# Tiles that 512-column products read moved to multiples of 1024 bytes, and the opening products of zeros taken out

## The chip, the cores and the metric

One core of a Trainium2 chip runs the whole program in one launch. The metric is the device time of one execution in microseconds (us); the median of three runs of the kernel before is 1070.89 us. The engines are named as the profile names them: PE (TensorE's matmuls), PEld (its weight loads), DVE (VectorE), ACT (ScalarE), POOL (GpSimd), SP (SyncE, which issues the DMAs).

## The reference

Three stages in float32, one after the other. B = 4, H = 8, S = 576, D = 64; 4 x 576 = 2304 tokens of 512 features; d_ff = 2048.

```python
scores = scale * np.matmul(q, k.transpose(0, 1, 3, 2))        # causal, softmax
local = np.matmul(a, v)
mem_out = mem_ret / mem_norm                                  # phi(q) @ M_prev over phi(q) . z_prev
x = g * mem_out + (1 - g) * local
...
h = x @ w_in;  r = np.maximum(h, 0.0);  y = (s * (r * r) + b) @ w_out      # first layer
...
h = y @ w_in2;  g = h * np.tanh(softplus(h));  out = g @ w_out2            # second layer
```

## The kernel before

Every large product is made of three: each operand is split into a high and a low float32r part, and hi*hi, hi*lo and lo*hi are added in PSUM. `W[layer, "wih"/"wil"/"woh"/"wol", r]` are the weights' parts (w_in high and low, w_out high and low), four tiles of 512 columns each.

- **Attention** makes x in units of one batch and head; scores are `a` tiles, L469 to L474, transposes L533, products with V L561.
- **First layer.** Tokens go in five blocks of 256 (`blocks1`, j = 0 to 4) and then two of 512 ("big"). `first` makes h = x @ w_in for one 128-wide slice fc of d_ff: 12 products through `mm_in` (L699), whose moving operand is `xh` or `xl` in a small block and `yh` or `yl` in a big one, and whose stationary operand is a slice of `wih` or `wil`. `y_part` (L763) multiplies the result, `gh` and `gl` (in a big block two halves of a tile that takes the rings `xh` and `xl`), moving, by slices of `woh` and `wol`, stationary, into the block's accumulators. A small block has two accumulators of one PSUM bank each, `y0` and `y1`, each holding two 256-column results; L759 opens each with a product of a tile of zeros over all its 512 columns. A big block has four accumulators.
- **Second layer.** Blocks of 512, 512, 512, 512 and 256 tokens (`blocks2`). `mish` makes h (L699 again, moving `yh` or `yl`, stationary `wih` or `wil`); ACT applies Mish, DVE splits the result into a tile `raw` (three slices of four) or `gg` (every fourth). `o_part` (L847) multiplies: stationary a 128-wide slice of `raw` or `gg`, moving 512 columns of `woh` or `wol`. On PE four products of h and four of o alternate.
- `column_sums` adds all of the first layer's w_out up on DVE (L672, L674), and one product with a tile of ones (L692) sums over the partitions; it gives a bias of the second layer.

The order of every engine's queue is found at build time by `Plan`, which simulates the steps with fixed costs and priorities. Buffers are slots of named rings; `yh`, `yl` have two slots each, number 0 in the pool `m2a` on the right-hand end of SBUF and number 1 in the pool `m2b` on the left. The first-layer big blocks and the second layer's blocks 0, 2 and 4 take slot 0; blocks 1 and 3 take slot 1. `raw` has three slots, all on the right; `gg` one, on the left. Until about 85 us `Plan` also puts fill products (`zero_product`, L940) into PE's idle time.

The few lines on the fill and on the opening of an accumulator:

```python
def zero_product():
    if not idle:
        idle.append(ps_y.tile([P, 512], F32, tag="y1_0", name="idle"))
    nc.tensor.matmul(idle[0][:, :256].rearrange("p (k n) -> p k n", n=P), zeros,
                     zeros.unsqueeze(1).to_broadcast([P, 2, P]), start=True, stop=True)
plan.fill = (7.0, 85.0, 0.12, zero_product)
```

Of the kernel before, what the change touches and what calls it, by code (L numbers as in the profile page):

```python
# [9 lines left out]
F32 = mybir.dt.float32  # L10
F32R = mybir.dt.float32r
# [3 lines left out]
AF = mybir.ActivationFunctionType  # L15
# [4 lines left out]
P = 128  # L20
# [3 lines left out]
PE, ACT, DVE, POOL, DMA = range(5)  # L24
# [26 lines left out]
def act_us(n, extra=0):  # L51
    return 0.094 + 0.00083 * n + 0.093 * extra


def dve_us(n, fast=False):
    return 0.068 + (0.00052 if fast else 0.00104) * n
# [61 lines left out]
class Plan:  # L118
# [29 lines left out]
    def add(self, engine, us, prio, f, r=(), w=(), after=(), keep=(), share=1.0):  # L148


        bufs = list({id(b): b for b in (*r, *w, *keep) if b.ring is not None}.values())
        new = [b for b in bufs if b.maker is None]
        waits = {id(s): s for b in r for s in b.writers}
        waits.update((id(s), s) for s in after)
        s = Step(engine, us, prio, f, list(waits.values()), bufs, new)
        s.share = share
        s.left = len(waits)
        for x in waits.values():
            x.next.append(s)
        for b in bufs:  # L160
            b.users += 1
            if b.maker is None:
                b.maker = s
            elif id(b.maker) not in waits:
                b.maker.next_start.append(s)
                s.left += 1
        for b in w:
            b.writers.append(s)
        self.steps.append(s)
        return s  # L170
# [100 lines left out]
def attention_then_two_ffn(ctx: ExitStack, tc: tile.TileContext, qk, qz, vm, beta,  # L271
# [3 lines left out]
    nc = tc.nc  # L275
    B, H = qk.shape[:2]
    NQ, D = qz.shape[3] - 1, qz.shape[4]
# [20 lines left out]
    add = plan.add  # L298

    const = ctx.enter_context(tc.tile_pool(name="const", bufs=1))  # L300
# [6 lines left out]
    mask = const.tile([P, SP], BF16, name="mask")  # L307
    nc.gpsimd.memset(mask[:, :SP - P], 0.0)
    make_causal_mask(nc, mask[:, SP - P:], MASKED)
    zeros = const.tile([P, P], F32R, name="zeros")  # L310
    ones = const.tile([P, P], F32, name="ones")
    igate = const.tile([P, 2, H], F32, name="igate")
    sb = const.tile([P, 2], F32, name="sb")
    bcs = const.tile([P, NCC], F32, name="bcs")
# [16 lines left out]
    nc.vector.tensor_scalar_min(igate[:, 1], igate[:, 1], 80.0)  # L331
    nc.scalar.activation(igate, igate, AF.Exp)
    nc.vector.tensor_scalar_add(igate, igate, 1.0)
    nc.scalar.copy(zeros, mask[:, :P])
    nc.scalar.activation(ones, mask[:, :P], AF.Copy, bias=1.0)


    ps_h = ctx.enter_context(tc.tile_pool(name="ps_h", bufs=1, space=PSUM))
    stage = ctx.enter_context(tc.tile_pool(name="stage", bufs=1, side="right"))
    first_layer = ExitStack()  # L340
    m1 = first_layer.enter_context(tc.tile_pool(name="m1", bufs=1))
# [6 lines left out]
    R = {}  # L348

    def rings(pool, after=None, fifo=True, **sizes):  # L350
        for nm, n in sizes.items():
            R.setdefault(nm, Ring(nm, fifo)).more(pool, n, after)
# [14 lines left out]
    def unit(b, h, prio, groups=(TA, TB), place=None):  # L367
# [47 lines left out]


        ex = Buf(R["ex"], [P, NQ, D])
        nm = Buf(R["nm"], [P, NQ])
        lo_t, n_t = tiles[0], len(tiles)
        mine = slice(lo_t, lo_t + n_t)  # L420

# [242 lines left out]

    def column_sums(prio, begin):

        total, ps = Buf(R["total"], [P, 512]), Buf(R["h"], [P, 512])

        def more(r, j, nm):
            x = W[1, nm, r].t[:, j, :].bitcast(F32)  # L670
            if r == j == 0 and nm == "wol":
                nc.vector.tensor_tensor(total.t, W[1, "woh", 0].t[:, 0, :].bitcast(F32), x, op=ALU.add)  # L672
            elif r + j:
                nc.vector.tensor_tensor(total.t, total.t, x, op=ALU.add)  # L674

        for r in range(NR):
            for j in range(FPR):
                def pair(r=r, j=j):
                    more(r, j, "woh")
                    more(r, j, "wol")  # L680

                add(DVE, dve_us(512) * (2 if r + j else 1), prio, pair, [W[1, "woh", r], W[1, "wol", r]] + [total] * (r + j > 0), [total],
                    after=[begin] * (r + j == 0))

        def pick():
            for ec in range(NCC):
                nc.vector.tensor_tensor_reduce(total.t[:, ec * P:(ec + 1) * P], ps.t[:, ec * P:(ec + 1) * P], ident, 1.0, 0.0,
                                               ALU.mult, ALU.add, bcs[:, ec:ec + 1])
            nc.vector.tensor_scalar(bcs, bcs, sb[:, 1:2], None, op0=ALU.mult)

        plan.steps[-1].lag = 12.0
        add(PE, 0.87, prio, lambda: nc.tensor.matmul(ps.t, ones, total.t, start=True, stop=True), [total], [ps])  # L692
        add(DVE, 1.0, prio, pick, [ps, total], [sums_in, total])

    def mm_in(ph, layer, xh, xl, fc, part):
# [54 lines left out]
    def y_part(j, fc, acc, t, gh, gl, gh_bufs, gl_bufs, prio):  # L750
        r, jj = fc // FPR, fc % FPR
        n = blocks1[j][1]
        big = n > N1
        per = 512 // n

        def y(part):
            if fc == 0 and part == 0 and not big:
                for a in acc:
                    nc.tensor.matmul(a.t.rearrange("p (k n) -> p k n", n=P), zeros,  # L759
                                     zeros.unsqueeze(1).to_broadcast([P, 4, P]), start=True, stop=False)  # L760
            x, nm = ((gh, "woh"), (gh, "wol"), (gl, "woh"))[part]
            for ec in range(NCC):
                nc.tensor.matmul(acc[ec // per].t[:, (ec % per) * n:(ec % per + 1) * n],  # L763
                                 W[1, nm, r].t[:, jj, ec * P:(ec + 1) * P], t(x),
                                 start=(big and fc == 0 and part == 0),
                                 stop=(fc == NFC - 1 and part == 2 and ec % per == per - 1))

        for part in range(3):
            need = [*(gl_bufs if part == 2 else gh_bufs), W[1, "wol" if part == 1 else "woh", r]]
            add(PE, 0.48 if not big else 0.908, prio, lambda part=part: y(part), need + (acc if fc or part else []), acc,  # L770
                keep=[gh[0]])
# [22 lines left out]
    m2a, m2b, ps_or, ps_ol = [], [], [], []  # L794
# [77 lines left out]
    for h in range(H):  # L872
        unit(0, h, PRE_A + STEP_A * h, (TA,), PLACE_A[h % 4])
    for h in range(H):
        unit(0, h, PRE_B + STEP_B * h, (TB,), PLACE_B[h])
    raws = [raw_buf(i // 8, i % 8) for i in range(len(pieces))]
    weight_bufs(1)
    start = 0.0
# [3 lines left out]
    for i in range(3 * H):  # L882
        unit(1 + i // H, i % H, UNIT0 + UNIT * i)

    opened = add(NONE, 0.0, 0.0, open_second, after=attention_steps)
    rings(m2a, opened, raw=1, yr=4, yh=1, yl=1, g=2, total=1)
    rings(ps_or, opened, o0=1, o1=1, o2=1, o3=1)
    seq = [(j, fc) for j in range(NB1) for fc in range(NFC)]

# [5 lines left out]
    for i in range(len(seq) + LAG1):  # L895
        if i < len(seq):
            j, fc = seq[i]
# [6 lines left out]
        if i >= LAG1:  # L904
            j, fc = seq[i - LAG1]
# [3 lines left out]
    for p in pieces:  # L909
        convert(2, CONV2, *p, Buf(R["raw"], [P, 1024], I32), [opened])  # L910
    column_sums(700.0, begin_sums)
    weight_bufs(2)
    closed = add(NONE, 0.0, 0.0, close_first, after=list(plan.steps))
# [8 lines left out]
    for i in range(len(seq) + LAG2):  # L922
        if i < len(seq):
            blk, fc = seq[i]
# [4 lines left out]
        if i >= LAG2:  # L929
            blk, fc = seq[i - LAG2]  # L930
# [4 lines left out]
    idle = []  # L935

    def zero_product():
        if not idle:
            idle.append(ps_y.tile([P, 512], F32, tag="y1_0", name="idle"))
        nc.tensor.matmul(idle[0][:, :256].rearrange("p (k n) -> p k n", n=P), zeros,  # L940
                         zeros.unsqueeze(1).to_broadcast([P, 2, P]), start=True, stop=True)

    plan.fill = (7.0, 85.0, 0.12, zero_product)
    with tc.manual_schedule():
        plan.run()
# [42 lines left out]
```

## Time and profile before

| | |
|---|---|
| median of 3 runs | 1070.89 us (1070.43 to 1073.95) |
| the profiled execution, its own time | 1072.33 us |
| span in its profile, first to last instruction | 1070.5 us |
| PE busy | 1041.9 us, 97% of the span, 6021 instructions |
| DVE, ACT, POOL busy | 665.2, 534.7, 217.0 us |

The span is what the profile's clocks run over; the execution's own time lies 1.8 us above it. A product's time in the profile is from its start to its modelled end, and successive products overlap; how fast PE goes is read from the starts of successive products, or from how many stand in a stretch in which PE has no idle time.

### The profile page before, as it was taken

How to read it: one execution, taken by the hardware profiler on the slowest of the kernel's cores; microseconds unless marked ns; L12 is line 12 of the kernel's file. 1: busy time of each engine (PE TensorE's matmuls, PEld its weight loads, DVE VectorE, ACT ScalarE, POOL GpSimd, SP SyncE). 2: the span in 40 equal slices, each digit the busy share in tenths (PEclk: the TensorE clock that was granted, in tenths of full speed). 3: DMA queues.
4: the chain of work that ended last, by engine and by line, in shares of the span. 5: the costliest groups of instructions: out<-in, count | busy, mean ns of one | idle time of the engine just before them, and what ended most of it. 6: DMA issues, size and time to landing. Idle time of an engine off the chain costs nothing.

```text
span 1070.5 us, 17570 instructions
## 1 busy us (share of the span) xinstructions
PE 1041.9 (97%) x6021; PEld 897.9 (84%) x6021; DVE 665.2 (62%) x1962; ACT 534.7 (50%) x1268; POOL 217.0 (20%) x337
## 2 busy tenths in 40 slices
PE   7999998999999999999999999999999999999998
PEld 5667787999999999998768878888888888888887
DVE  7899999999999999856986565422311322222122
ACT  6887896878788888755345454312111211111111
POOL 5753443333223332213233200000000000000000
PEclk9999999999999999999999999999999999999999
DMA  8654552334323332267366754200200100010010
GB/s 268 180 171 142 172 180 80 113 103 137 94 86 90 122 93 82 67 191 209 121 190 192 245 188 148 79 1 2 77 1 1 42 19 1 0 40 1 1 40 20
DMA packets 52073, 106.66 MB, mean 100 GB/s; under 512 B 6672, under 2 KB 27664, under 8 KB 51984
## 3 DMA queue, kind: packets, MB, share of 16 engines
q1 hardware_dynamic: 51552, 105.54, 31.7%
q8 instruction: 47, 0.77, 0.3%
q14 instruction: 42, 0.34, 0.1%
q10 hardware_dynamic: 432, 0.01, 0.0%
HBM read 82.97 MB, written 22.54 MB: 99 GB/s over the span
## 4 chain that ended last, share of the span: by engine, by line
PE 76%; DVE 11%; DMA 3%; issue 2%; ACT 2%; POOL 1%; SPq 0%; DVEq 0%; ACTq 0%; POOLq 0%
PE h L699 31%; PE o L847 19%; PE y L763 10%; PE a L561 5%; PE a L533 4%; PE o L763 3%; PE a L473 2%; PE a L474 2%; DVE total L674 2%; DMA raw<-w_in_d 1%; DVE w L637 1%; DVE w L636 1%; DMA w_out_d<-w 1%; DVE Pt L478 1%; POOL w L639 1%
## 5 line engine op out<-in xcount | busy, mean ns | idle before, releaser
L836 ACT ACTIVATE g<-h 128x512 f32<-128x512 f32 (+1 forms) x80 | 44.5, 556 | 319.7 <-PE h L699 297.4
L837 DVE CAST raw<-g 128x512 fp32r<-128x512 f32 (+1 forms) x60 | 24.0, 401 | 214.5 <-ACT g L836 166.4
L847 PE MATMUL o<-woh,raw 128*128 128x512 f32 x432 | 119.2, 394 | 0.0
L699 PE MATMUL h<-yh,wih 128*128 128x512 f32 (+1 forms) x448 | 115.0, 379 | 3.1 <-DVE g L743 3.1
L699 PE MATMUL h<-yh,wil 128*128 128x512 f32 (+1 forms) x448 | 114.7, 378 | 0.0
L699 PE MATMUL h<-yl,wih 128*128 128x512 f32 (+1 forms) x448 | 114.7, 378 | 0.0
L639 POOL TENSOR_TENSOR w<-w,raw 128x512 int32<-128x512 int32 x54 | 75.0, 1388 | 163.9 <-DVE w L637 123.2
L699 PEld LDWEIGHTS h<-yh,wih 128*128 128x128 f32 x448 | 81.3, 188 | 22.3 <-DVE g L743 5.2
L490 POOL TENSOR_SCALAR Pt<-ex,nm 128x64 f32<-128x64 f32 x148 | 72.1, 500 | 126.6 <-DVE nm L439 64.9
L699 PEld LDWEIGHTS h<-yl,wih 128*128 128x128 f32 x448 | 81.7, 188 | 17.5
L699 PEld LDWEIGHTS h<-yh,wil 128*128 128x128 f32 x448 | 81.7, 188 | 17.5
L847 PEld LDWEIGHTS o<-woh,raw 128*128 128x128 f32 x432 | 79.2, 188 | 17.0
L487 ACT ACTIVATE Pt<-Pt,mx 128x64 f32<-128x64 f32 (+4 forms) x148 | 81.7, 553 | 20.7 <-DVE mx L478 20.2
L533 PE MATMUL a<-ident,Pt 128*128 128x128 f32 x432 | 66.1, 280 | 5.9 <-POOL Pt L504 2.4
L541 DVE TENSOR_TENSOR PTl<-a,PTh 128x128 fp32r<-128x128 f32 (+1 forms) x144 | 63.9, 481 | 1.0 <-ACT PTh L538 0.6
L478 DVE CUSTOM_DVE_ANT_0 Pt<-a,mask 128x320 f32<-128x320 f32 (+3 forms) x148 | 59.8, 419 | 7.4 <-PE a L469 4.2
L847 PE MATMUL o<-wol,raw 128*128 128x512 f32 x216 | 59.8, 394 | 0.0
L533 PEld LDWEIGHTS a<-ident,Pt 128*128 128x128 f32 x432 | 50.0, 143 | 10.8 <-POOL Pt L504 4.6
L538 ACT CAST PTh<-a 128x128 fp32r<-128x128 f32 (+1 forms) x144 | 54.3, 433 | 5.8 <-PE a L533 4.8
L699 PE MATMUL h<-xh,wih 128*128 128x256 f32 x320 | 52.0, 287 | 2.8 <-DVE rt L743 2.7
L763 PE MATMUL y<-gh,wol 128*128 128x256 f32 x320 | 53.1, 288 | 0.0
L763 PE MATMUL y<-gl,woh 128*128 128x256 f32 x320 | 53.0, 288 | 0.0
(195 smaller groups left out, 2327.8 us busy)
## 6 DMA issues: line engine op xcount, KB each, us to landing
qk<-in_qk SPq DMA_DIRECT2D x24, 608.0 KB, 3.8
raw<-in_w_out SPq DMA_DIRECT2D x28, 512.0 KB, 3.9
raw<-in_w_in SPq DMA_DIRECT2D x26, 512.0 KB, 4.7
qn<-in_qz SPq DMA_DIRECT2D x29, 192.0 KB, 2.4
vx<-in_vm SPq DMA_DIRECT2D x29, 160.0 KB, 2.4
out<-ot SPq DMA_DIRECT2D x18, 256.0 KB, 2.1
w_in_d<-w SPq DMA_DIRECT2D x16, 256.0 KB, 3.2
w_out_d<-w SPq DMA_DIRECT2D x16, 256.0 KB, 3.4
```

Of the source, the lines that this page charges most:

```text
L478: nc.vector.tensor_tensor_reduce(Pt[t].t[:, D + lo:D + hi], ps.t[:, :hi - lo], mask[:, SP - w + lo:SP - w + hi], -SCALE, mx.t[:, t:t + 1] ...
L487: nc.scalar.activation(Pt[t].t[:, D:w + D], Pt[t].t[:, D:w + D], AF.Exp, bias=mx.t[:, t + i:t + i + 1], scale=-1.0, accum_out=rs.t[:, t:t ...
L490: add(POOL, 0.3, lambda: nc.gpsimd.tensor_scalar(Pt[t].t[:, :D], ex.t[:, t, :], nm.t[:, t:t + 1], 1.0, op0=ALU.mult, op1=ALU.mult), [ex, n ...
L533: nc.tensor.transpose(ps.t[:, c - c0, :], Pt[t].t[:, c * P:(c + 1) * P], ident)
L538: (nc.vector.tensor_copy if dve else nc.scalar.copy)(PT[0].t[:, at_], ps.t[:, :n])
L541: nc.vector.tensor_tensor(PT[1].t[:, at_], ps.t[:, :n], PT[0].t[:, at_].bitcast(F32), op=ALU.subtract)
L561: nc.tensor.matmul(o.rearrange("p (t q) -> p t q", q=P), v, x.t[:, f[0]:f[-1] + 1:f[1] - f[0] if len(f) > 1 else 1, :], start=(c == 0 and ...
L639: add(POOL, 1.23, prio, lambda: nc.gpsimd.tensor_tensor(w.t, w.t, words()[:, :, 0], op=ALU.add), [raw, low_words, w], [w])
L699: nc.tensor.matmul(ph, W[layer, nm, r].t[:, cc, o:o + P], x[:, cc], start=(part == 0 and cc == 0), stop=(part == 2 and cc == NCC - 1))
L763: nc.tensor.matmul(acc[ec // per].t[:, (ec % per) * n:(ec % per + 1) * n], W[1, nm, r].t[:, jj, ec * P:(ec + 1) * P], t(x), start=(big and ...
L836: add(ACT, act_us(n) + 0.06, ew, lambda: nc.scalar.activation(g.t, ph.t[:, :n], AF.Mish), [ph], [g])
L847: nc.tensor.matmul(acc[i].t, gg.t[:, k, i * P:(i + 1) * P], W[2, nm, r].t[:, jj, :], start=(fc == 0 and part == 0), stop=(fc == NFC - 1 an ...
```

## The change

Where tiles lie. `zeros` and `ones` (512 bytes each) leave the constants, so that everything on the left-hand end moves down by 1024 bytes; a pool `edge` of 992 bytes is put at the right-hand end, and `nm` grows from 20 to 64 bytes. Start addresses per partition in the two built programs, as the remainder of a division by 1024:

| tiles | before | after |
|---|---|---|
| weights, `xh`, `xl`, `gh`, `gl`, `gg`, slot 1 of `yh` and `yl` (left) | 0 | 0 |
| slot 0 of `yh` and `yl`, `raw` (three slots), `yr`, `g`, `total`, `w32` (right) | 992 | 0 |
| attention's `PTh`, `PTl` | 992, 480 | 0, 512 |
| attention's `B1`, `B2` | 736, 736 | 768, 768 |

The products of zeros. L759 is gone; instead the first product into each bank of a small block has start set, and the second half of the bank is written by a product without it. The fill products multiply the bfloat16 mask's zero columns instead of a float32r tile of zeros. The tile of ones is made by ACT just before it is used, in the pool `m2a`.

```diff
-    zeros = const.tile([P, P], F32R, name="zeros")
-    ones = const.tile([P, P], F32, name="ones")
...
-    nc.scalar.copy(zeros, mask[:, :P])
-    nc.scalar.activation(ones, mask[:, :P], AF.Copy, bias=1.0)
...
+    edge = ctx.enter_context(tc.tile_pool(name="edge", bufs=1, side="right"))
+    edge.tile([P, 248], F32, name="edge")
     stage = ctx.enter_context(tc.tile_pool(name="stage", bufs=1, side="right"))
...
-        nm = Buf(R["nm"], [P, NQ])
+        nm = Buf(R["nm"], [P, 16])
...
-        total, ps = Buf(R["total"], [P, 512]), Buf(R["h"], [P, 512])
+        total, ps, ones = Buf(R["total"], [P, 512]), Buf(R["h"], [P, 512]), Buf(R["ones"], [P, 2 * P])
...
-        add(PE, 0.87, prio, lambda: nc.tensor.matmul(ps.t, ones, total.t, start=True, stop=True), [total], [ps])
+        add(ACT, act_us(P), prio, lambda: nc.scalar.activation(ones.t[:, :P], mask[:, :P], AF.Copy, bias=1.0), [], [ones], after=[begin])
+        add(PE, 0.87, prio, lambda: nc.tensor.matmul(ps.t, ones.t[:, :P], total.t, start=True, stop=True), [total, ones], [ps])
...
         def y(part):
-            if fc == 0 and part == 0 and not big:
-                for a in acc:
-                    nc.tensor.matmul(a.t.rearrange("p (k n) -> p k n", n=P), zeros,
-                                     zeros.unsqueeze(1).to_broadcast([P, 4, P]), start=True, stop=False)
...
-                                 start=(big and fc == 0 and part == 0),
+                                 start=(fc == 0 and part == 0 and ec % per == 0),
...
-    rings(m2a, opened, raw=1, yr=4, yh=1, yl=1, g=2, total=1)
+    rings(m2a, opened, raw=1, yr=4, yh=1, yl=1, g=2, total=1, ones=1)
...
-        nc.tensor.matmul(idle[0][:, :256].rearrange("p (k n) -> p k n", n=P), zeros,
-                         zeros.unsqueeze(1).to_broadcast([P, 2, P]), start=True, stop=True)
+        nc.tensor.matmul(idle[0][:, :256], mask[:, :P], mask[:, :256], start=True, stop=True)
```

The queues of DVE, POOL and SP hold the same instructions in the same order before and after. On PE, this is the opening of the second small block's accumulators (j = 1) before; names are out<-moving,stationary, and h, y are PSUM tiles:

```order
L699 MATMUL h_2550<-xl_2223,wih_0_802 128x256 x4
L699 MATMUL h_2622<-xh_2070,wih_0_802 128x256 x4
L759 MATMUL y_0_2632<-zeros 128x512
L759 MATMUL y_0_2633<-zeros 128x512
L763 MATMUL y_0_2632<-gh_2483,woh_0_483 128x256 x2
L763 MATMUL y_0_2633<-gh_2483,woh_0_483 128x256 x2
```

and now (the lines have moved up by one or two):

```order
L698 MATMUL h_2548<-xl_2221,wih_0_802 128x256 x4
L698 MATMUL h_2620<-xh_2068,wih_0_802 128x256 x4
L758 MATMUL y_0_2630<-gh_2481,woh_0_483 128x256 x2
L758 MATMUL y_0_2631<-gh_2481,woh_0_483 128x256 x2
L531 MATMUL a_2639<-ident,Pt_0_2412 128x128 x4
```

The two products of zeros are gone, in each of five such places, and nothing else on PE has changed its place. On ACT, this is the stretch in which the column sums are made, before:

```order
L629 ACTIVATE w_0_7898<-raw_7823 128x512
L742 ACTIVATE g_7905<-h_7865 128x512
L634 ACTIVATE raw_7871<-raw_7871 128x512
L629 ACTIVATE w_1_7929<-raw_7871 128x512
L745 CAST xh_7945<-g_7905 128x512
```

and now:

```order
L627 ACTIVATE w_0_7888<-raw_7813 128x512
L741 ACTIVATE g_7895<-h_7855 128x512
L690 ACTIVATE ones_7898<-mask 128x128
L632 ACTIVATE raw_7861<-raw_7861 128x512
L627 ACTIVATE w_1_7921<-raw_7861 128x512
L744 CAST xh_7937<-g_7895 128x512
```

The one ACT step for the ones has moved here from the program's start, where the copy that made the zeros has gone with it.

## Rows read from the trace of the kernel before

**Rows 1.** Page: busy time, share of the span and instructions; the chain's shares.

```profile
PE 1041.9 (97%) x6021; PEld 897.9 (84%) x6021; DVE 665.2 (62%) x1962; ACT 534.7 (50%) x1268; POOL 217.0 (20%) x337
...
PE 76%; DVE 11%; DMA 3%; issue 2%; ACT 2%; POOL 1%; SPq 0%; DVEq 0%; ACTq 0%; POOLq 0%
```

**Rows 2.** Busy time by stretch (start:end, length, engines with counts, PE's clock, DMA).

```profile
17.00:84.60 67.60, 61.60 (x339) 43.95 (x339) 60.19 (x215) 57.53 (x152) 43.25 (x64) 0.97 0.64 194
...
84.60:173.00 88.40, 80.82 (x546) 67.47 (x545) 84.18 (x254) 72.25 (x174) 37.68 (x49) 1.00 0.48 153
173.00:477.60 304.60, 303.68 (x2469) 300.27 (x2468) 279.28 (x1068) 241.06 (x660) 84.38 (x174) 0.99 0.35 105
477.60:505.00 27.40, 27.40 (x142) 23.24 (x141) 14.26 (x26) 14.36 (x27) 8.79 (x7) 1.00 0.74 213
505.00:556.00 51.00, 47.62 (x201) 37.07 (x200) 47.76 (x69) 22.40 (x37) 15.03 (x10) 1.00 0.50 146
556.00:604.00 48.00, 47.78 (x204) 38.43 (x205) 29.62 (x54) 25.78 (x44) 15.17 (x11) 1.00 0.72 231
604.00:639.00 35.00, 35.00 (x151) 27.99 (x149) 20.88 (x25) 17.98 (x26) 4.14 (x3) 1.00 0.55 182
639.00:660.50 21.50, 21.31 (x93) 17.39 (x93) 12.65 (x17) 12.01 (x18) 0.00 (x0) 1.00 0.41 133
660.50:1071.00 410.50, 406.35 (x1853) 334.06 (x1851) 106.04 (x194) 62.46 (x110) 0.00 (x0) 1.00 0.07 26
```

**Rows 3.** Timeline of PE, second layer, block 1, products of o from gg.

```profile
759.07 1.07 PE L699 MATMUL h<-yh,wih 128*128 128x512 f32 x4
759.98 1.07 PE L847 MATMUL o<-woh,gg 128*128 128x512 f32 x4
760.88 1.07 PE L699 MATMUL h<-yh,wil 128*128 128x512 f32 x4
...
764.51 1.98 PE L699 MATMUL h<-yh,wih 128*128 128x512 f32 x8
```

**Rows 4.** The same, block 1, products of o from raw.

```profile
790.17 1.09 PE L847 MATMUL o<-wol,raw 128*128 128x512 f32 x4
...
795.69 0.63 PE L847 MATMUL o<-wol,raw 128*128 128x512 f32 x2
```

**Rows 5.** The same, block 0, products of o from raw.

```profile
723.81 1.10 PE L699 MATMUL h<-yl,wih 128*128 128x512 f32 x4
...
728.48 0.86 PE L847 MATMUL o<-wol,raw 128*128 128x512 f32 x3
```

**Rows 6.** Timeline of PE, first layer, beginning of the second big block.

```profile
570.13 1.10 PE L699 MATMUL h<-yh,wil 128*128 128x512 f32 x4
...
576.63 0.63 PE L763 MATMUL o<-xh,woh 128*128 128x512 f32 x2
```

**Rows 7.** Timeline of PE at the opening of small block 1.

```profile
188.48 0.64 PE L699 MATMUL h<-xh,wih 128*128 128x256 f32 x4
188.96 0.62 PE L759 MATMUL y<-zeros 128*128 128x512 f32 x2
189.42 0.64 PE L763 MATMUL y<-gh,woh 128*128 128x256 f32 x4
```

**Rows 8.** The chain that ended last, around 636 us (start, us, what).

```profile
630.17 5.38 DMA raw<-w_in_d
...
636.71 1.05 DVE wil L662
...
638.54 0.61 DVE g L743
```

**Rows 9.** Waits of PE, 173 to 477 us (total, times, longest).

```profile
PE h L699 <- DVE rt L743: 0.5, 1, 0.5
```

**Rows 10.** The fill products alone by stretch (PE, PEld, clock, DMA).

```profile
17.00:84.60 67.60, 17.16 (x105) 13.93 (x104) 0.97 0.64 194
```

**Rows 11.** Timeline of ACT at the start.

```profile
4.79 0.30 ACT L335 ACTIVATE ones<-mask 128x128 f32<-128x128 bf16 x1
```

## The prediction

> **What bounds the kernel now.** I read the page's busy line and chain first: PE is busy 97% of the span, and the chain that ended last runs through PE for 76% of it and through DVE for 11% [rows 1]. An average hides stages, so next the busy times by stretch [rows 2]. The reader is to see four kinds. To 173 us PE is idle for 6.0 us of 67.6 and for 7.6 us of 88.4, while DVE is busy 84.18 of the latter 88.4: DVE's work orders that stage, and PE time saved there is worth nothing. From 173 to 477.6 PE is idle for 0.9 us of 304.6. From 477.6 to 660.5 the first layer's two big blocks run, and inside them two stretches where PE is not what ends last: 505 to 556, with DVE busy 47.76 us of 51 (the column sums beside the second layer's weights), and 604 to 639, where the chain runs through the reloading of weights, DMA, ACT, DVE, up to the step of DVE that PE waits for [rows 8]. From 660.5 to its last product PE has no idle time at all: 1853 products in 406.35 us.
>
> So the question is how far apart successive products start where PE never waits. That is read from timelines, in groups of four products (a row's own time is longer, as products overlap). In the second layer's block 1 its operands, slot 1 of `yh` and `yl`, begin at remainder 0 of 1024; where the stationary tile is `gg` (0 too) six groups take 764.51 - 759.07 = 5.44 us, 0.907 us each, 227 ns a product [rows 3]. With `raw` (remainder 992) stationary, in the same block, six groups take 795.69 - 790.17 = 5.52, 0.920 each [rows 4]. In block 0, whose `yh`, `yl` are slot 0 (992), five groups from 723.81 to 728.48 take 4.67, 0.934 each [rows 5]. Same code, same shapes, same clock; PE is never idle in the three. What differs is which tiles lie at 992.
>
> **The change part by part.**
>
> *Second layer.* If every tile at remainder 0 brings the pace of [rows 3], 1661 of the 1853 products (512 columns) take 226.7 ns; the other 192, block 4's h, have 256 columns and take 0.12 us (a group of four at 256 columns takes 188.96 - 188.48 = 0.48 [rows 7]). That makes 376.6 + 23.0 = 399.6 us against 406.35 [rows 2]. Of the difference some 0.2 us is the last product's own tail, which stays. Gain 6.6 us, all on the path: ACT is busy 62 and DVE 106 us of this stretch and have room.
>
> *First layer, big blocks.* `yh`, `yl` are slot 0; the products of y move `xh`, `xl` (0) past weights (0) between them. Seven groups from 570.13 to 576.63 take 6.50, 0.929 each [rows 6]; at 0.907 each saves 0.022 us. Two blocks of 16 slices with six groups make 192 groups: 4.2 us. In the 86 us of 505 to 556 and 604 to 639 I count the saving as lost to the waits named above, in the other 97 of 183 us as gained: 2.2 us. The bounds are 0.7 us (the second stretch also swallows what is saved ahead of it) and 4.2 us (both waits begin earlier by what PE saves).
>
> *Small blocks.* Products with 256 columns are left at 0.12 us; I give them nothing. Five pairs of products of zeros go, 189.42 - 188.96 = 0.46 us a pair [rows 7]. The first pair, at 84 us, lies where DVE orders the work: 0. The other four are worth 1.84 us at most. Ahead of the fourth PE waits 0.5 us for DVE [rows 9], which may take back what the second and third give: bounds 0.9 and 1.84, I take 1.4. The first real product into the bank now has start set and waits for what the zeros waited for; no wait is added.
>
> *The ones and zeros on ACT.* Two steps leave the start, 0.30 us each at most [rows 11]; one such step comes back in 505 to 556, where ACT is busy 22.40 of 51 us [rows 2], so that its idle time hides it; without that cover it would cost 0.30 us. I take 0 for both, with bounds -0.3 and +0.3.
>
> *Fill products.* 105 of them between 17 and 84.6 us, 17.16 us of PE [rows 10]. They stand where PE would idle, so their own length costs nothing. In bfloat16 they carry a weight load of their own, as the profile already counts one for each. Not shown by the trace is whether they hold the clock; that is a rival below.
>
> *Attention* reads `B1`, `PTh` at other addresses, most products with 384 columns or fewer. No row separates their pace by address, and to 173 us DVE covers what they take: 0.
>
> The sum is 6.6 + 2.2 + 1.4 = 10.2 us. The profiled execution took 1072.33 us, so 1062.1; the median of the runs is 1.44 us below that execution, which makes 1060.7 us.
>
> One rule speaks against the whole of it. The Trainium skill, "TensorE: Matmul & The Clock Gate", section "Wait — 56ns, not 53.3ns?", has the start-to-start time of warm products as the columns over 2.4 GHz plus about 2.5 ns, 215.7 ns at 512 columns, and where the operand lies does not enter. The trace disagrees on the figure (227 ns at best [rows 3]) and on its being one figure (0.907, 0.920, 0.934 us for four). By that rule the addresses would be worth 0 and the sum 1.4 us; by the rows it is 10.2.
>
> **The rivals.** (A) As above. (E) The same pace, but the two waits in the big blocks move up with PE and all four later zero pairs count: 6.6 + 4.2 + 1.84 = 12.6 us, 1058.2 us. For it: much of what DVE does there itself follows PE. Against it: DVE's 47.76 of 51 us.
>
> (B) Only the moving operand's address counts, and what separates [rows 3] from [rows 4] is something else about `gg`, such as its place on the left. Then block 1's pace with `raw`, 0.920, is what all reach: the second layer's blocks 0 and 2 gain 0.014 us in each of 192 groups, 2.7 us; the big blocks at 0.920 gain 0.009 in 192, half of it kept, 0.9; with the zeros 5.0 us, 1065.9. Against it: in [rows 3] and [rows 4] block and moving tiles are the same.
>
> (C) It is not the remainder but the place: slot 1 and `gg` lie on the left, slot 0 and `raw` on the right, and after the change they still do. The trace before can't part the two, since every tile on the right is at an odd remainder and every one on the left is not. Then only the zeros count: 1.4 us, 1069.5, which can't be told from no change. For it: no row here speaks against it. Against it, weakly: a moving tile [rows 5] and a stationary one [rows 4] show the loss alike, in three different slots on the right, and the one thing that these share with no faster tile, besides their side, is the remainder. The page's rule above would end here too.
>
> (D) Slower: the bfloat16 fill does not hold the clock. It has one place, 17 to 84.6 us, where the granted clock is 0.97 of full [rows 2]. PE's real work there is 61.6 - 17.2 = 44.4 us; at the lower level (1.2 GHz) it takes at most 44.4 us more, of which fill and idle time, 17.2 + 6.0 us, take up 23.2: +21.2 us at worst, 1060.7 + 21.2 = 1081.9. It turns the gain of 10.2 into a loss once PE is at the lower level for about half of that stage. Against it: the products are as many, of as many columns, at the same places in the queue.
>
> **How the numbers follow.** Chances: A 0.60, E 0.08, B 0.13, C 0.13, D 0.06. The likeliest is A, 1060.7 us, its own range 1058.9 (waits that move) to 1062.7 (bounds of the big blocks and zeros). No change that a measurement of this kernel tells is within 0.3%, 3.2 us: 1067.7 to 1074.1. A, E and B are faster by more than that, C is within it, D (in the cases that reach half of the stage) slower; a small part of D stays within. So faster 0.81, same 0.14, slower 0.05. The range from 1057.5 to 1066.5 holds A, E and B, 0.81, and leaves out C and D.
>
> **What would show it right or wrong.** In the changed kernel's timeline groups of four should start 0.907 us apart in blocks 0 and 1 alike, with `raw` and with `gg`, so that 400 us are enough for the products after the first layer. If block 0 has 0.920, B; if 0.934, C. The fill's granted clock to 84.6 us settles D. In the big blocks PE's waits at 505 to 556 and near 639 should be longer than before by about what the products save there (1.2 and 0.8 us by 0.022 us a group); if they are not, E. Between 173 and 477 us the stretch should be 1.4 us shorter; PE's wait for DVE ahead of the fourth opening tells the rest. The prediction is wrong if right-hand tiles keep their pace.

## The result and the profile after

The changed kernel takes 1061.68 us (median of 4 runs, 1059.61 to 1064.32); the kernel before, run beside it, 1072.28 us. The ratio is 0.9901, 95% interval 0.9884 to 0.9919: 10.6 us less, where 10.2 had been summed and 1060.7 us forecast. The profiled execution took 1059.81 us, its span is 1058.0 us against 1070.5. Ratios compare the executions in the faster of two states; one of the four of the kernel `sums_cost` below, at 2611 us, is not in its ratio.

The page of the changed kernel, busy time and chain, answers to [rows 1]:

```profile
PE 1027.7 (97%) x6011; PEld 891.4 (84%) x6011; DVE 665.0 (63%) x1962; ACT 533.4 (50%) x1267; POOL 218.5 (21%) x337
...
PE 47%; DMA 0%; DVE 0%; ACT 0%; issue 0%; ACTq 0%
```

PE is still what bounds it; the chain could be followed back over less of the span this time, so its shares are not compared. Busy times by stretch of the changed kernel (start:end, length, engines with counts, clock, DMA); the first is the early stage, the next two are the big blocks, whose first products stand at 474.3, 564.9 and, as the second layer's first, 654.7 us (counted off in PE's order):

```profile
17.00:84.60 67.60, 60.15 (x342) 40.08 (x341) 61.02 (x217) 57.38 (x153) 44.02 (x64) 0.97 0.64 192
...
474.30:564.90 90.60, 85.91 (x392) 69.86 (x391) 70.38 (x114) 44.49 (x78) 27.98 (x20) 1.00 0.59 179
564.90:654.70 89.80, 89.80 (x398) 74.39 (x397) 55.44 (x75) 48.12 (x74) 14.85 (x11) 1.00 0.60 194
...
654.70:1058.50 403.80, 399.62 (x1853) 334.19 (x1851) 105.94 (x194) 62.31 (x110) 0.00 (x0) 1.00 0.07 26
```

The last row answers to the last of [rows 2]: the same 1853 products take 399.62 us instead of 406.35. The pace itself is in PE's timeline, here in the second layer's block 0 with `raw` stationary, which answers to [rows 5] (0.934 us a group of four there):

```profile
715.42 1.07 PE L842 MATMUL o<-wol,raw 128*128 128x512 f32 x4
716.33 1.07 PE L698 MATMUL h<-yl,wih 128*128 128x512 f32 x4
717.24 1.07 PE L842 MATMUL o<-woh,raw 128*128 128x512 f32 x4
...
720.86 0.39 PE L842 MATMUL o<-wol,raw 128*128 128x512 f32 x1
```

Six groups take 720.86 - 715.42 = 5.44 us, 0.907 each, to the hundredth what [rows 3] had. The opening of small block 1, as in [rows 7]:

```profile
187.25 0.64 PE L698 MATMUL h<-xh,wih 128*128 128x256 f32 x4
187.73 0.65 PE L758 MATMUL y<-gh,woh 128*128 128x256 f32 x4
188.22 1.03 PE L531 MATMUL a<-ident,Pt 128*128 128x128 f32 x8
```

By stage, from the starts of the same products in both profiles:

| from, to the first product of | before | after | less |
|---|---|---|---|
| start, small block 1 | 158.8 us | 157.6 | 1.2 |
| small block 1, first big block | 318.8 | 316.7 | 2.1 |
| first big block, second | 90.7 | 90.6 | 0.1 |
| second big block, second layer | 92.2 | 89.8 | 2.4 |
| second layer, last product | 405.9 | 399.3 | 6.6 |

The stages add up to 12.4 us, about what separates the two profiled executions (1072.33 and 1059.81 us). The medians are 10.6 us apart: executions of one kernel differ by several us (1059.61 to 1064.32 here), and the profiled one is among the shortest. So a difference of 1 or 2 us in one of the upper rows is not by itself an effect of the change; the second layer takes 405.9 us in a second profile of the kernel before too.

### The profile page after: what moved, and what is told of

It reads as the page before. It is cut to its first block, busy times and chain, and to the rows that moved or that the text cites. A ratio compares the mean times of both kernels' runs of the same rounds, so it can differ in the third digit from the quotient of the medians.

```text
span 1058.0 us, 17549 instructions
## 1 busy us (share of the span) xinstructions
PE 1027.7 (97%) x6011; PEld 891.4 (84%) x6011; DVE 665.0 (63%) x1962; ACT 533.4 (50%) x1267; POOL 218.5 (21%) x337
```

## The experiments

That the right-hand tiles now run at 0.907 ends the rivals B and C as they stood. But it leaves open *what* of an address counts: the tile's own start (theory A), or the distance between the tile that moves and the one that is loaded as weights (theory R), which the kernel before also had off by 32 bytes. Of the first four kernels two part the change into its pieces, and two, with the left-hand end or both ends off by 32 bytes, were made for that question.

In all of them the pace is read from two stretches of 70 us in which PE is never idle, one in block 0 (665 to 735 us) and one in block 1 (750 to 820); the count of products is some two more than 70 us over the pace, as those cut by an edge count too. The kernel before, then the changed one:

```profile
665.00:735.00 70.00, 70.00 (x302) 1.00 0.12 42
750.00:820.00 70.00, 70.00 (x307) 1.00 0.08 28
```

```profile
665.00:735.00 70.00, 70.00 (x311) 1.00 0.09 31
750.00:820.00 70.00, 70.00 (x311) 1.00 0.04 16
```

So 302 is 0.934 us a group of four, 307 is 0.920, 311 is 0.907.

**Only the zeros gone, in the kernel before.**

```diff
-                for a in acc: nc.tensor.matmul(..., zeros, ..., start=True, stop=False)
-                                 start=(big and fc == 0 and part == 0),
+                                 start=(fc == 0 and part == 0 and ec % per == 0),
```

> The kernel before with one edit: the five pairs of products of zeros are gone; every address, the fill products and the two early ACT steps stay as before. Theory A (the start remainder sets the pace, the zeros are a separate 1.4 to 1.84 us): the pace stays at 0.934 us a group of four in block 0 and 0.920 in block 1, and the time is 1.4 to 1.9 us below the kernel before, ratio about 0.9985. To 74 us it should run like the kernel before, since fill and ACT steps are the old ones. Rival (the zeros' removal by itself shifts the whole plan, and the changed kernel's gain is mostly that): 5 us or more, ratio below 0.996.

Measured: ratio 0.9973 (0.9961 to 0.9985), some 2.9 us. The pace is that of before:

```profile
665.00:735.00 70.00, 70.00 (x303) 1.00 0.09 31
750.00:820.00 70.00, 70.00 (x307) 1.00 0.05 19
```

From small block 1 to the first big block it takes 474.6 - 158.7 = 315.9 us against 318.8. That is more than the 1.84 us of the four pairs. PE's wait of 0.5 us at 352 us [rows 9] is not there. The ratio expected was 0.9985, so the zeros are worth about twice that here (1.6 to 4.2 us by the interval), and still less than the 5 us of the rival.

**The right-hand pool taken out again.**

```diff
-    edge = ctx.enter_context(tc.tile_pool(name="edge", bufs=1, side="right"))
-    edge.tile([P, 248], F32, name="edge")
```

> The changed kernel without the 992-byte pool at the right-hand end, so that the right-hand tiles begin at remainder 992 of 1024 again; all else as changed. Theory A: 6.6 us of the second layer and 2.2 to 2.6 of the big blocks go back, block 0 at 0.934 and block 1 at 0.920 a group again, about 1069 to 1070 us, ratio about 0.998. Rival (left end moved by 1024 bytes, or something else in the change, sets the pace): it stays near 1060.

Measured: 0.9987 (0.9976 to 0.9998), and the old pace:

```profile
665.00:735.00 70.00, 70.00 (x302) 1.00 0.12 41
750.00:820.00 70.00, 70.00 (x308) 1.00 0.08 29
```

So the faster pace hangs on the 992 bytes alone; the move of the left-hand end by 1024 bytes does nothing for it. This kernel gains less than the one with only the zeros gone (0.9987 against 0.9973, intervals that overlap); its small block 1 begins at 161.5 us against 158.7, which is taken up under the start and the fill.

**The left-hand end off by 32 bytes.**

```diff
+    const.tile([P, 8], F32, name="off")
-        nm = Buf(R["nm"], [P, 16])
+        nm = Buf(R["nm"], [P, NQ])
```

> The changed kernel with the left-hand end moved by 32 bytes (one more 32-byte constant; the two small attention tiles get their 20 bytes back to make room): weights, xh, xl, gh, gl, gg, slot 1 of yh and yl at remainder 32, the right-hand tiles at 0. Theory A in its absolute form (each tile's own start counts): every 512-column product now has a moving or a stationary operand off the multiple, o loses most as its moving tiles are weights; block 0 and block 1 at 0.920 to 0.934 a group, 6 to 10 us lost against the changed kernel, ratio to before 0.997 to 1.0. Rival R (what counts is the distance between moving and stationary tile, which is off by 32 in the kernel before too): the same loss here. Rival C (right-hand place): no loss, ratio 0.990.

Measured: 0.9985 (0.9973 to 0.9998).

```profile
665.00:735.00 70.00, 70.00 (x303) 1.00 0.12 43
750.00:820.00 70.00, 70.00 (x307) 1.00 0.08 29
```

This speaks against theory A. Block 1 reads slot 1 of `yh` and `yl` and the weights, all on the left, all at remainder 32, and its products of h should have suffered; but its pace is the 0.920 of the kernel before, in which they were all at 0. What is slow is again what joins left and right. In both kernels the right-hand tiles stand 32 bytes below the left-hand ones (992 is 32 short of 1024), and kind by kind the groups of four in blocks 0 and 1 take the same time on average, to 1 ns.

**Both ends off by 32 bytes.**

```diff
+    const.tile([P, 8], F32, name="off")
-    edge.tile([P, 248], F32, name="edge")
+    edge.tile([P, 240], F32, name="edge")
```

> The changed kernel with both ends moved by 32 bytes: every tile that a 512-column product reads begins at remainder 32, so that the distances between moving and stationary tiles are multiples of 1024 as in the changed kernel. Theory A, absolute: slower than either one-sided case, 0.934 a group or more in all blocks, ratio about 1.000 to 1.005. Rival R (the distance counts): 0.907 a group everywhere, ratio 0.990.

Measured: 0.991 (0.9889 to 0.9931), the changed kernel's ratio within the intervals.

```profile
665.00:735.00 70.00, 70.00 (x311) 1.00 0.09 31
750.00:820.00 70.00, 70.00 (x311) 1.00 0.04 16
```

Not one of the tiles that a 512-column product reads begins at a multiple of 1024 here (nor of 64), and the pace is 0.907 everywhere. Theory A is wrong in its absolute form: the distance between the tiles counts. The second layer, from its first product to its last, takes 405.9 us in the kernel before and with the left-hand end alone moved, and 399.3 us in the changed kernel and here.

**Which distances.** The right-hand tiles at remainder 64, 128 and 256, the left-hand ones at 0 (the pool has 232, then 216 and 184 words):

```diff
-    edge.tile([P, 248], F32, name="edge")
+    edge.tile([P, 232], F32, name="edge")
```

> The changed kernel with the right-hand pool 64 bytes shorter, so that right-hand tiles begin at remainder 64 of 1024 and left-hand ones at 0. Theory R (the distance between a product's moving tile and the stationary tile counts, and 32 bytes too many is what hurts) leaves the unit open. If the unit is 64 bytes: 0.907 us a group of four everywhere, 394 us of PE from 660.5 on. If it is 1024 (or anything over 64): 0.934 in block 0 and 0.920 in block 1, as with remainder 992, and about 6.6 us more in the second layer.

> The same with the right-hand tiles at remainder 256. Unit 64, 128 or 256: 0.907 a group everywhere. Unit 512 or 1024: 0.934 and 0.920.

> The changed kernel with the right-hand tiles at remainder 128 of 1024. Theory R with a unit of 128 bytes: 0.907 us a group of four in all blocks, PE done with 1828 to 1842 products from 660.5 us on at 227 ns each. With a unit of 256: slower groups in blocks 0 and 1, about as with remainder 64.

At remainder 64, then 128, then 256:

```profile
665.00:735.00 70.00, 70.00 (x303) 1.00 0.09 33
750.00:820.00 70.00, 70.00 (x305) 1.00 0.05 18
```

```profile
665.00:735.00 70.00, 70.00 (x303) 1.00 0.11 40
750.00:820.00 70.00, 70.00 (x305) 1.00 0.07 23
```

```profile
665.00:735.00 70.00, 70.00 (x310) 1.00 0.09 31
750.00:820.00 70.00, 70.00 (x310) 1.00 0.04 16
```

Distances of 64 and 128 bytes are as bad as 32 (one time each: 1070.7 and 1072.03 us; second layer 406.3 and 406.2 us), a distance of 256 is free (1063.06 us; 399.3 us). So the unit is neither 64 nor 128 bytes; a multiple of 256 bytes fits all runs. The bad distance of 32 was tried with the right-hand tiles below the left-hand ones only, those of 64 and 128 with them above. Distances such as 192 or 384 were not tried.

**Which operand.** Only two slots of `raw` at 992; then only the pool of slot 0 of `yh` and `yl` and of the third `raw`. A pad stands ahead of `m2a` in `open_second`; in the first kernel it has 248 words and the pool `edge` is gone, in the second 8 words and `edge` stays:

```diff
+        off = ctx.enter_context(tc.tile_pool(name="off", bufs=1, side="right"))
+        off.tile([P, 248], F32, name="off")
```

> The changed kernel with only two of the three slots of raw at remainder 992 (the right-hand end as before; a pad of 992 bytes brings the pool of yh, yl and the third raw back to 0). Theory R: h in all blocks and o from gg and from the third raw at 0.907, o from the two other slots slower; in block 0 and in block 1 alike groups average 0.91 to 0.915, some 2 to 3 us lost in the second layer, nothing in the big blocks. Rival B of the prediction (only the moving operand's address counts): 0.907 everywhere.

> The changed kernel with only the pool of slot 0 of yh and yl and of the third raw at remainder 992 (a pad of 32 bytes ahead of it); two raw slots at 0. Theory R: blocks 0 and 2 and the big blocks lose what they gained (0.92 to 0.93 a group), blocks 1 and 3 stay near 0.907 but for every third raw; some 3.5 to 4.5 us lost in the second layer and 2 in the big blocks.

The chain of the first (start, us, what), in block 1:

```profile
773.91 0.93 PE o L842 x4
774.84 0.91 PE h L696 x4
775.75 0.91 PE o L842 x4
...
785.72 0.91 PE h L696 x4
786.63 0.93 PE o L842 x4
```

Groups of o go at 0.93 while `raw` is one of the two displaced slots, at 0.91 in the `gg` and the third-`raw` groups between, and at 0.93 again. So the stationary tile's address counts as well as the moving one's (rival B fails by itself). Its two stretches hold 309 and 308 products, and its second layer takes 401.5 us, 2.2 more than the changed kernel's, where 2 to 3 were expected.

When it counts can be read from PEld, the weight loads, in block 1 of the kernel before (the second name behind the arrow is the tile that is loaded):

```profile
786.29 0.87 PEld L847 LDWEIGHTS o<-woh,gg 128*128 128x128 f32 x4
787.19 0.87 PEld L699 LDWEIGHTS h<-yh,wil 128*128 128x128 f32 x4
788.10 0.89 PEld L847 LDWEIGHTS o<-woh,raw 128*128 128x128 f32 x4
789.03 0.87 PEld L699 LDWEIGHTS h<-yl,wih 128*128 128x128 f32 x4
789.94 0.89 PEld L847 LDWEIGHTS o<-wol,raw 128*128 128x128 f32 x4
790.87 0.87 PEld L699 LDWEIGHTS h<-yh,wih 128*128 128x128 f32 x4
```

```profile
788.33 1.09 PE L847 MATMUL o<-woh,raw 128*128 128x512 f32 x4
```

The first load of `raw` starts at 788.10 us, 0.23 us, which is one product, ahead of the first product that uses it (788.33). The groups of loads follow each other by 0.93 us where `raw` is loaded and by 0.90 to 0.91 where `gg`, `wih` or `wil` is. So in this block PE is slow in just those products during which a tile at a bad distance from the one that they move is being loaded for the next product: the last h ahead of a group with `raw`, and the first three o of that group. The 0.920 of [rows 4] is an average over both. In block 0 it does not come out so cleanly: there groups of o with `gg` take 0.918 to 0.927 us, though everything that they move or load lies at remainder 0. Between slow groups some of the loss goes over to products at a good distance; why is not shown.

In the second kernel it is the other way about:

```profile
665.00:735.00 70.00, 70.00 (x303) 1.00 0.09 31
750.00:820.00 70.00, 70.00 (x310) 1.00 0.04 16
```

Block 0, which moves slot 0, is back at the old pace; block 1 is hardly touched. Its second layer takes 404.3 us, 5.0 more than the changed kernel's (3.5 to 4.5 were expected), its second big block 91.8 us against 89.8. One time each: 1062.55 and 1067.74 us.

**The kernel before, profiled again.**

> The kernel before, once more, for its profile. If the 0.5 us that PE waits for DVE at 352 us, ahead of the fourth opening, belongs to the kernel (the zeros delay what DVE evacuates), the wait is there again. If it is how one DMA happened to land (DVE waited 0.46 us for the write of ys), it is gone or elsewhere, and the stretch from 173 to 477 us is shorter by about as much. The pace of the groups should be as in the first profile: 0.934 and 0.920.

Its waits of PE from 173 to 478 us hold the same row at the same place:

```profile
PE h L699 <- DVE rt L743: 0.5, 1, 0.5
```

and the stretch from small block 1 to the first big block took 478.9 - 160.5 = 318.4 us. The wait is there in both profiles of the kernel with the zeros, and in none of the kernels without them, but for the one with more fill, whose order is another.

**Two tries at the waits that are left.** In the changed kernel PE waits for DVE in the first big block, where its column sums run. In one kernel the planner's cost of their adds is raised; in the other all planned idle time of PE to 85 us is filled.

```diff
-                add(DVE, dve_us(512) * (2 if r + j else 1), prio, pair, ...
+                add(DVE, 1.0 * (2 if r + j else 1), prio, pair, ...
```

```diff
-                        int(now / self.TICK + 1e-9) > self.tick or self.count < 1.5 * self.ENOUGH):
+                        True):
```

> The changed kernel with one cost of the planner changed: an add of the column sums is planned at 1.0 us instead of 0.60, nearer to the adds of up to 1.7 us that the trace shows. The tensors computed are the same. If PE's waits from 520 to 556 us (some 6 us) come of DVE falling behind its plan with the sums, the sums spread further, PE waits less and 2 to 4 us come off, ratio about 0.987. If DVE's work there is simply too much, the waits move and the time stays at the changed kernel's, ratio 0.990.

> The changed kernel with the fill put into all of PE's planned idle time to 85 us (166 products instead of 121). If the spread of times of one kernel comes of the granted clock in 17 to 84.6 us (0.92 to 0.97 in the profiles so far, the first block starting at 72.7 to 76.5 us), more fill holds it nearer to 1.0 and the median falls by 1 to 2 us. If the fill itself delays the products that the attention waits for, the first block starts later and the time grows by up to 45 x 0.11 = 5 us.

The sums' cost: ratio 0.9854 (0.983 to 0.9879) to the kernel before, with a span of 1056.1 us, below the changed kernel. PE's waits between 478 and 660 us were, in the changed kernel,

```profile
PE h L698 <- DVE g L742: 3.6, 3, 1.5
PE h L691 <- DVE g L742: 1.1, 1, 1.1
```

and there are none in this one; its first big block, from 478.6 to 562.0 us, has PE busy all through and takes 83.4 us instead of 90.6 (the second takes 90.7 instead of 89.8). The row begins 0.6 us ahead of it:

```profile
478.00:562.00 84.00, 84.00 (x395) 70.35 (x394) 66.58 (x100) 41.37 (x73) 23.93 (x17) 1.00 0.56 167
```

The fill: 0.9936 (0.9916 to 0.9955), above the changed kernel's 0.9901 with intervals that just meet: the median does not fall. Its early stage is the one that has the full clock throughout:

```profile
17.00:84.60 67.60, 65.35 (x383) 43.32 (x382) 60.11 (x216) 55.49 (x149) 42.29 (x63) 1.00 0.64 200
```

but small block 1 begins at 166.9 us and the first big block at 479.9, against 157.6 and 474.3 us in the changed kernel's profile. Between 84 and 478 us PE waits 7.7 us for DVE's step `rt` there, against 2.6; in the two big blocks it waits no longer than in the changed kernel (4.3 against 4.7 us). The filled order is another plan, so that its loss is not put down to the fill's own length alone.

## Why the prediction was right, point by point

**The sum: right, and closer than it deserves.** 10.2 us were summed and the medians are 10.6 apart. Between the two first profiles the three terms of the sum come to 6.6, 2.5 and 2.1, and 1.2 more at the start that no term had. Against the second profile of the kernel before (`before_again`), the same three are 6.6, 2.1 and 1.7. The second layer's term is firm. In the big blocks two errors cancel, and both smaller terms change by 0.4 to 0.5 us with the profile that they are taken from, so that the sum's last half microsecond is luck.

**Second layer: right in size, wrong in its reason.** 6.6 us were summed and 6.6 came; 399.6 us were worked out for the 1853 products and 399.62 measured. The step "if every tile at remainder 0 brings the pace of [rows 3]" gave the right number because equal remainders of 1024 make every distance a multiple of 256. As a rule it is wrong: with both ends at remainder 32 the pace is the same. I saw that the rows could not part side from remainder; I did not see that they could not part remainder from distance either, since one side was at 0 in every row.

**Big blocks: 2.2 summed, 2.5 measured, and the split was wrong.** I lost 505 to 556 and 604 to 639 and kept the rest. The whole first block is lost (90.7 to 90.6 us): PE's idle time in it grew from 90.7 - 87.1 = 3.6 to 4.7 us, about the 1.2 us that were named for this wait (but the kernel with only the zeros gone has 4.6 us there at the old pace). Over all runs that keep the planner's costs and the fill this block takes 90.2 to 91.7 us at the old pace and 90.1 to 90.7 at the new one; what sets its length is the DVE queue with the column sums, as `sums_cost` shows, which spreads them and needs 83.4 us. The second block keeps all that its products save, 2.4 us (2.0 against `before_again`), where 96 groups at 0.022 make 2.1. The step that failed is to count 604 to 639 as lost. The wait there [rows 8] was no fixed limit: PE's idle time at its end was 0.19 us in the first profile,

```profile
639.20 1.19 PE L699 MATMUL h<-yh,wih 128*128 128x512 f32 x4 [0.19 <-DVE g L743]
```

and in `before_again`, with the old pace and the zeros, PE has none in the whole block:

```profile
569.60:661.40 91.80, 91.80 (x397) 74.39 (x396) 55.07 (x75) 47.83 (x74) 15.15 (x11) 1.00 0.59 189
```

Too much kept in the first block and too little in the second: two errors that cancel, which is luck. Rival E is right for the second block and wrong for the first.

**Small blocks: 1.4 summed, 2.1 measured, above the bound of 1.84 (1.7 against `before_again`).** The term mis-sized is "which may take back what the second and third give". The wait at 352 us does not take back, it goes: with the zeros alone removed the stretch is 2.9 us shorter than in the first profile and 2.5 shorter than in the second. The 1.84 us of the pairs and the 0.5 us of the wait make most of that. In the kernels without zeros that keep the changed kernel's plan, the stretch takes 314.7 to 317.1 us, so one profile does not give this term to better than about 1 us. Why DVE comes in time there once the zeros are gone is not settled.

**The start and the fill: 0 summed, 1.2 us seen, not settled.** The first product of small block 1 stands at 157.6 us in the changed kernel, but in two profiles of the kernel before at 158.8 and 160.5, and in kernels with the changed fill anywhere from 157.6 to 162.2 (166.9 in the one with more of it). Neither the shorter fill nor the ACT steps can be told from that spread. It goes with the granted clock of the stretch from 17 to 84.6 us, which ranges from 0.92 to 0.97 over these profiles: small block 1 begins at 157.6 to 158.8 us where it is 0.97, at 160.1 and 160.5 where it is 0.94, and at 161.1 to 162.2 where it is 0.92. The kernel with the fill of zeros in float32r has a lower one too, here in its second profile:

```profile
17.00:84.60 67.60, 61.81 (x324) 42.41 (x323) 58.65 (x212) 55.41 (x148) 41.62 (x63) 0.94 0.65 196
```

Rival D as it was priced, half of the stage or more at the lower level, did not come: 0.97 before, 0.97 after. A small part of it stays open. Of the ten profiles with the bfloat16 fill (and no more of it than before) five show 0.92, a value that none of the three with the float32r fill has (0.97, 0.94, 0.97); three are too few to say whether the fill has a part in that.

**The rule of the Trainium skill** ("TensorE: Matmul & The Clock Gate", section "Wait — 56ns, not 53.3ns?") knows no address. The trace disagrees with it twice: 227 ns at best for a 512-column float32r product where the formula of the Trainium skill gives 215.7, and 230 to 234 ns on average where tiles stand at a bad distance. So the sum by that rule, 1.4 us, fell too.

## What to carry to other kernels

Where products follow each other without a gap, compare the pace of the same product from different buffers before looking for idle time: here up to 3% of a stretch in which PE was never idle could be saved (0.934 to 0.907 us a group). For products like these, 512 float32r columns with a weight load each, lay the tiles that a product moves and those loaded as weights at distances of a multiple of 256 bytes. One 32-byte tile at one end was enough to lose the pace, and a common remainder (0 and 32 were tried) was enough to have it. And ask of a correlation in the rows which other quantity moves with it: shifting everything by the same 32 bytes took one more kernel and overturned the rule that the number had seemed to prove.

## What the runs showed of the hardware that was not expected

- The pace of 512-column float32r products depends on the distance between the start of the moving tile and that of the stationary one: 0.907 us for four at a distance of 0 or 256 bytes (modulo the 512 bytes by which the slices of one tile are spaced), 0.92 to 0.934 at 32, 64 and 128. In block 1 of the kernel before the slow products are those during which the next product's weights are loaded from a bad distance (groups of loads 0.93 us apart, the others 0.90 to 0.91). So a moving tile and the weights loaded beside it get into each other's way; by what means, and why in block 0 products at a good distance are slow too, is not shown.
- Products with 256 columns lose next to nothing at the bad distance. In the small blocks, at distance 0, four take 0.48 us [rows 7]; in the second layer's last block, where the kernel before moves slot 0 (992) past weights at 0, its chain has

```profile
1062.19 0.47 PE h L699 x4
```

  and the 336 products of that block, the 144 of o with 512 columns among them, take 55.8 us from the first start to the last, against 55.6 in the changed kernel.

- One price in the planner, 0.60 us for DVE's adds, was worth some 5 us (0.9901 to 0.9854), more than the products of zeros (0.9973 alone): an order made from the lower price let DVE fall behind, and PE waited.
